# Zero rows under short k and v tiles, a third result buffer, and a new order of first loads in a linear-attention and softplus kernel

## The chip, the cores and the metric

The kernel runs on one NeuronCore of a Trainium2 chip. The metric is the device time of one execution in microseconds (us), the median of several runs. The engines are called PE (TensorE), DVE (VectorE), ACT (ScalarE), POOL (GpSimd) and SP (SyncE, which issues the DMA transfers).

## The reference

```python
batch, n_heads, seq, head_dim = (8, 8, 576, 64)

def attn(q, k, v, g_norm):
    kv = np.einsum('bhsd,bhse->bhde', k, v)
    out = np.einsum('bhsd,bhde->bhse', q, kv)
    rms = np.sqrt(np.mean(out * out, axis=-1, keepdims=True) + 1e-06)
    return out / rms * g_norm

def moe(x, w_in, w_out):                 # 4608 tokens, 512 -> 2048 -> 512
    h = x @ w_in
    g = np.maximum(h, 0.0) + np.log1p(np.exp(-np.abs(h)))
    return g @ w_out
# x is attn's output as (batch*seq, heads*dim); w_in and w_out are float64
```

A batch has 576 rows, that is four times 128 and 64 more. These 64 are the "tail" below.

## The kernel before

The program is written as tasks with an engine, an assumed duration, what they follow, which buffers of a ring they take and give back, and a priority number `pos`. Before anything is emitted, a list planner plays the tasks through with the assumed durations and fixes the order of every engine's queue:

```python
first = min(at for at, _ in options)
at, t = min(((at, t) for at, t in options if at <= first + self.SOON),
            key=lambda o: (o[1].pos, o[0]))        # the smallest pos among those that can start soon
```

On the chip each queue is worked off in that order.

The priorities of the first loads and conversions come from one list of 24 numbers:

```python
P0 = [-16.0, -13.7, -11.8, ...]
CONVERT, FETCH, EARLY = P0[:8], P0[8:16], P0[16:]
```

The sum over rows of k by v, per batch, with the tail as its last group:

```python
for p in range(NP + 1):
    ks, vs = slot("kvt"), slot("kvt")
    tail = p == NP
    ...
            if tail:
                l, r = pairs(ks.tile[:n], i), vs.tile[:n, 2 * i:2 * i + 2]     # n = 64
            else:
                l, r = pairs(ks.tile, i), vs.tile.rearrange("s (h i) d -> s h i d", h=2)[:, :, i]
            nc.tensor.matmul(kv[:, i if tail else p], lhsT=l, rhs=r, ...)
    last = add("PE", 1080 if tail else 820, run, ...)
```

After the attention rows come 192 steps (12 blocks of 384 tokens by 16 blocks of the hidden size, in three phases). Each step has 12 products `h`, a softplus, and 9 products `s`. Float32 factors are split in three parts for accuracy. At the end of a block the result tiles leave:

```python
ot = slot("xg" if ph == 0 else "qT")       # a ring of two
```

## Time and profile before

| | before |
|---|---|
| median, 3 runs | 940.94 us |
| median, the 6 runs timed with the changed kernel | 941.95 us |
| span of the profiled run | 942.6 us |
| PE busy | 921.1 us |
| PE idle ahead of the last matmul, of it ahead of the first | 16.2 us, 9.0 us |
| last matmul to the end | 5.2 us |

PE is the bound, and the lines of it stand in the prediction. To read them: "L544" is a line of the program, `h<-xv,w` gives the written and read tiles, and a fp32 matmul of the program shows as two instructions, so the four products of a k-by-v group are "x8".

### The profile page before, as it was taken

To read this page: it belongs to the slowest core of one execution; us is meant where nothing else is said; L and a number is where in the kernel's file an instruction comes from. 1 tells how busy PE (TensorE), PEld (TensorE's weight loads), DVE (VectorE), ACT (ScalarE), POOL (GpSimd) and SP (SyncE) were. 2 spreads that over 40 slices of the span, in tenths; PEclk is the share of its full clock that TensorE was granted. 3 is DMA by queue.
4 is the path that set the end of the run, shared out by engine and by line. 5 is a ranking of instruction groups with operands and counts; after the bars stand their busy time and mean duration, and the time that the engine had idled before them with its cause. 6 is when DMAs were issued, how large, how long until landed. Compare 5 with 4: busy or idle time off the path is not lost.

```text
span 942.6 us, 13502 instructions
## 1 busy us (share of the span) xinstructions
PE 921.1 (98%) x4978; PEld 834.6 (89%) x4978; DVE 597.9 (63%) x1043; ACT 447.7 (47%) x871; POOL 66.7 (7%) x42
## 2 busy tenths in 40 slices
PE   4899999999999999999999999999999999999997
PEld 3799899998989899899899999999999999999996
DVE  7788876677777646677666666485455454544452
ACT  6777666665565554544443333374323323233231
POOL 0322212122222000000000000000000000000000
PEclk9899999999999999999999999999999999999999
DMA  9998778857654433433333343343333322322321
GB/s 241 230 254 226 208 211 227 231 172 217 188 180 156 145 124 123 146 123 114 137 121 122 125 141 102 135 146 101 101 101 101 101 101 102 101 82 83 98 72 68
DMA packets 148673, 135.63 MB, mean 144 GB/s; under 512 B 86400, under 2 KB 102784, under 8 KB 148608
## 3 DMA queue, kind: packets, MB, share of 16 engines
q1 hardware_dynamic: 148448, 134.78, 47.0%
q8 instruction: 39, 0.64, 0.4%
q14 instruction: 26, 0.21, 0.1%
q10 hardware_dynamic: 160, 0.00, 0.0%
HBM read 93.85 MB, written 40.89 MB: 143 GB/s over the span
## 4 chain that ended last, share of the span: by engine, by line
PE 96%; DMA 2%; SPq 1%; DVE 0%; ACT 0%; issue 0%; POOL 0%; DVEq 0%; POOLq 0%
PE h L544 42%; PE s L551 42%; PE o L458 4%; PE o L482 3%; PE tp L498 2%; PE tp L476 2%; DMA x<-xg 1%; DMA q<-in_q_dram 1%; DMA kvt<-in_v_dram 1%; PE s L482 0%; SPq L442 0%; DMA out_dram<-qT 0%; POOL r L490 0%; SPq L444 0%; PE h L343 0%
## 5 line engine op out<-in xcount | busy, mean ns | idle before, releaser
L551 PE MATMUL s<-w,gv 128*128 128x512 f32 x1728 | 438.0, 396 | 0.3 <-ACT xg L585 0.3
L544 PE MATMUL h<-xv,w 128*128 128x384 f32 x2304 | 435.2, 337 | 0.0
L544 PEld LDWEIGHTS h<-xv,w 128*128 128x128 f32 x2304 | 405.0, 188 | 14.0
L551 PEld LDWEIGHTS s<-w,gv 128*128 128x128 f32 x1728 | 318.4, 188 | 59.1 <-ACT xg L585 0.6
L564 ACT ACTIVATE g<-h 128x384 f32<-128x384 f32 x192 | 94.2, 491 | 381.3 <-PE h L544 381.0
L555 DVE TENSOR_TENSOR gv<-g,gv 128x384 fp32r<-128x384 f32 x192 | 106.6, 555 | 180.2 <-ACT gv L566 179.6
L559 DVE SCALAR_TENSOR_TENSOR gv<-gv 128x384 fp32r<-128x384 f32 x192 | 107.0, 557 | 5.5
L566 ACT ACTIVATE gv<-g 128x384 fp32r<-128x384 f32 x192 | 100.9, 525 | 5.2
L400 DVE TENSOR_TENSOR xv<-xt,xv 128x512 fp32r<-128x512 f32 x102 | 70.1, 688 | 25.6 <-ACT xv L397 25.3
L490 POOL TENSOR_TENSOR r<-r,half 128x8 f32<-128x8 f32 x36 | 66.0, 1834 | 233.5 <-DVE r L487 233.5
L397 ACT ACTIVATE xv<-xt 128x512 fp32r<-128x512 f32 x102 | 63.6, 624 | 29.7 <-DMA xt<-x 29.7
L403 DVE SCALAR_TENSOR_TENSOR xv<-xv 128x512 fp32r<-128x512 f32 x108 | 74.5, 690 | 2.9
L458 PE MATMUL o<-kvt,kvt 128*128 128x128 f32 (+1 forms) x320 | 46.2, 290 | 10.9 <-DMA kvt<-in_v_dram 10.8
L458 PEld LDWEIGHTS o<-kvt,kvt 128*128 128x128 f32 (+1 forms) x320 | 42.9, 202 | 15.0 <-issue 13.3
L591 DVE SCALAR_TENSOR_TENSOR qT<-s,scale,kvt 128x512 f32<-128x512 f32 x36 | 26.9, 749 | 44.7 <-PE s L551 29.8
L591 DVE SCALAR_TENSOR_TENSOR qT<-s,kvt 128x512 f32<-128x512 f32 x36 | 24.8, 688 | 33.9 <-PE s L551 25.9
L482 PE MATMUL o<-kv_diag,qT 128*128 128x128 f32 (+1 forms) x296 | 37.0, 277 | 0.0
L482 PEld LDWEIGHTS o<-kv_diag,qT 128*128 128x128 f32 (+1 forms) x296 | 34.3, 179 | 1.2 <-issue 1.0
L486 DVE TENSOR_REDUCE r<-x 128x8 f32<-128x512 f32 x36 | 24.6, 685 | 14.1 <-ACT x L506 13.8
L501 ACT COPY qT<-tp 128x512 f32<-128x512 f32 x36 | 21.0, 583 | 18.8 <-PE tp L476 18.6
L512 ACT ACTIVATE xg<-tp,g_col 128x512 f32<-128x512 f32 x36 | 24.7, 686 | 9.0 <-PE tp L498 8.2
L493 DVE TENSOR_TENSOR x<-o,r 128x512 f32<-128x512 f32 x33 | 22.7, 687 | 7.0 <-POOL r L490 6.7
(61 smaller groups left out, 456.2 us busy)
## 6 DMA issues: line engine op xcount, KB each, us to landing
xt<-x SPq DMA_DIRECT2D x102, 256.0 KB, 3.3
kvt<-part SPq DMA_DIRECT2D x72, 256.0 KB, 4.0
kvt<-in_k_dram SPq DMA_DIRECT2D x72, 128.0 KB, 3.9
x<-xg SPq DMA_DIRECT2D x36, 256.0 KB, 3.1
part<-xg SPq DMA_DIRECT2D x36, 256.0 KB, 3.3
part<-qT SPq DMA_DIRECT2D x36, 256.0 KB, 2.1
out_dram<-qT SPq DMA_DIRECT2D x36, 256.0 KB, 3.1
raw<-in_moe_w_in_dram SPq DMA_DIRECT2D x16, 512.0 KB, 5.1
```

The source lines that it names most:

```text
L397: nc.scalar.activation(cols(0, F32R), x.tile, func=AF.Copy, scale=DOWN)
L400: nc.vector.tensor_tensor(out=cols(1, F32R), in0=x.tile, in1=cols(0), op=ALU.subtract)
L403: nc.vector.scalar_tensor_tensor(out=cols(2, F32R), in0=cols(1), scalar=-RADIX, in1=cols(0), op0=ALU.mult, op1=ALU.add)
L458: nc.tensor.matmul(kv[:, i if tail else p], lhsT=l, rhs=r, start=(p == 0 and i == 0), stop=tail, skip_group_check=True)
L482: nc.tensor.matmul(pairs(y[r0:r0 + n], p), lhsT=qT.tile[:, p, r0:r0 + n], rhs=kv_diag[b % 2][:, p], start=(p == 0), stop=True, skip_group_ ...
L490: nc.gpsimd.tensor_tensor(out=r.tile, in0=r.tile, in1=half, op=ALU.pow)
L544: nc.tensor.matmul(hp, lhsT=w_in.tile[:, i, kd * P:(kd + 1) * P], rhs=xv.tile[:, i, kd], start=(m == 0), stop=(m == 3 * KD - 1))
L551: nc.tensor.matmul(mine[i].tile, lhsT=gv.tile[:, m, i * P:(i + 1) * P], rhs=w_out.tile[:, m], start=(c == cs[0] and m == 0), stop=(c == cs ...
L555: nc.vector.tensor_tensor(out=gv.tile[:, 1], in0=g.tile, in1=gv.tile.bitcast(F32)[:, 0], op=ALU.subtract)
L559: nc.vector.scalar_tensor_tensor(out=gv.tile[:, 2], in0=f32[:, 1], scalar=-RADIX, in1=f32[:, 0], op0=ALU.mult, op1=ALU.add)
L564: a = add("ACT", 490, lambda: nc.scalar.activation(new(g, [P, NT]), h.tile, func=AF.Softplus, scale=1.0 + E), [a], s, [g], [h])
L566: a = add("ACT", 530, lambda: nc.scalar.activation(new(gv, [P, 3, NT], F32R)[:, 0], g.tile, func=AF.Copy, scale=DOWN), [a], s, [gv])
```

## The change

The intent: the tail's tiles get buffers of their own whose lower 64 rows are zero, so that all products have 128 rows; the last phase gets three result buffers in place of two, by borrowing from two idle rings; and the 24 priorities are chosen anew. The core of the diff (cuts at "..."):

```diff
-    P0 = [-16.0, -13.7, -11.8, -9.7, -5.1, 0.0, -13.9, 2.7, -33.5, -33.3, -24.2, -17.7, -12.2, -10.2, 15.3, -2.2, 1.5, -10.5, 6.5, 7.0, 5.0, 4.0, 4.5, 6.5]
+    P0 = [-61.0, -9.7, -13.3, -2.2, -4.6, 5.5, -46.9, 0.2, -37.5, -33.8, -28.2, -10.7, -14.2, -13.7, 28.3, -2.7, 1.0, -9.0, 6.5, 7.0, 7.0, 20.0, -0.5, 2.5]
+    tails = [const.tile([P, H, D], F32, name=f"tail{i}") for i in range(2)]
+                 tail0=1, tail1=1, ...                       # two more rings
-            d4 = add("DVE", 430, power, [d3], pos, [p])
+            d4 = add("DVE", 430, power, [d3], pos, [p, w])
-            ready = add("DVE", 690, total, [d3, d5], pos, [w], [t, p])
+            ready = add("DVE", 690, total, [d3, d5], pos, [], [t, p])
-            ks, vs = slot("kvt"), slot("kvt")
+            ks, vs = (slot(f"tail{i}" if tail else "kvt") for i in range(2))
...
-                        l, r = pairs(ks.tile[:n], i), vs.tile[:n, 2 * i:2 * i + 2]
+                        l, r = pairs(ks.tile, i), vs.tile[:, 2 * i:2 * i + 2]
-            last = add("PE", 1080 if tail else 820, run, lds + [last], pos + 0.5 * p,
+            last = add("PE", 820, run, lds + [last], pos + 0.5 * p,
-        ot = slot("xg" if ph == 0 else "qT")
+        ot = slot("xg" if ph == 0 else ("qT", "x", "q")[t % TB] if ph == LAST else "qT")
-    for kvd in kv_diag:
-        nc.vector.memset(kvd, 0.0)
+    for x in kv_diag + tails:
+        nc.vector.memset(x, 0.0)
```

More of the change, by code (lines that the diff above doesn't have):

```diff
@@ L190 @@
     rings = dict(xv=2, gv=3, g=2, raw=2, lf=1, sq=2, t=1, p=1, w=1,
-                 xt=2, kvt=6, q=2, qT=2, x=2, xg=2, r=2,
+                 tail0=1, tail1=1, xt=2, kvt=6, q=2, qT=2, x=2, xg=2, r=2,
                  h=2, o=2, tp=1, s0=1, s1=1, s2=1)
@@ L429, in kv_of @@
         for p in range(NP + 1):
-            ks, vs = slot("kvt"), slot("kvt")
             tail = p == NP
+            ks, vs = (slot(f"tail{i}" if tail else "kvt") for i in range(2))
             n = S - MAIN if tail else P
             def load(src, s, p=p, tail=tail, n=n, ks=ks):
+                if tail:
+                    s.tile = tails[s is not ks]
+                    nc.sync.dma_start(out=s.tile[:n], in_=src[b, :, MAIN:].rearrange("h s d -> s h d"))
+                    return
                 x = new(s, [P, H, D])
-                if tail:
-                    nc.sync.dma_start(out=x[:n], in_=src[b, :, MAIN:].rearrange("h s d -> s h d"))
-                    return
                 src = src[b, 2 * p:2 * p + 2, :MAIN].rearrange("h (s i) d -> s h i d", i=4)
```

## The prediction

> **What bounds the kernel now.** I read the page first, then TensorE's waits, then a table of stretches, then the chain of waits in order of time at the places that the change touches.
>
> The page's head:
>
> ```profile
> PE 921.1 (98%) x4978; PEld 834.6 (89%) x4978; DVE 597.9 (63%) x1043; ACT 447.7 (47%) x871; POOL 66.7 (7%) x42
> ...
> PE 96%; DMA 2%; SPq 1%; DVE 0%; ACT 0%; issue 0%; POOL 0%; DVEq 0%; POOLq 0%
> ```
>
> TensorE (PE) is busy for 921.1 of 942.6 us, and it makes up 96% of the chain that ended last. A busy PE alone would not prove a bound, but the chain agrees. So the change can win in three ways only: fewer PE nanoseconds, less of the 942.6 - 921.1 = 21.5 us in which PE stands idle, or less PE work done at a low clock. Where those lie, the table of stretches says (I cut it at PE's first matmul, at the changes of the granted clock and at the first matmul of the main loop; columns: PE, PE weight loads, DVE, ACT, POOL, clock, DMA share, GB/s):
>
> ```profile
> 0.00:8.96 8.96, 0.00 (x1) 0.03 (x1) 5.29 (x13) 5.16 (x9) 0.70 (x6) 1.00 0.75 209
> 8.96:14.30 5.34, 4.75 (x18) 3.96 (x18) 4.95 (x9) 2.32 (x6) 0.00 (x0) 1.00 1.20 281
> 14.30:21.20 6.90, 3.64 (x22) 2.65 (x22) 5.35 (x9) 6.10 (x13) 0.00 (x0) 1.00 1.27 249
> 21.20:31.40 10.20, 9.92 (x39) 8.56 (x40) 5.45 (x11) 5.78 (x13) 1.28 (x1) 0.50 1.18 269
> 31.40:44.50 13.10, 10.28 (x82) 8.90 (x80) 12.32 (x23) 10.75 (x21) 6.27 (x4) 1.00 0.79 206
> 44.50:75.00 30.50, 30.50 (x207) 28.19 (x206) 24.75 (x46) 21.91 (x45) 5.41 (x4) 1.00 0.99 241
> 75.00:300.00 225.00, 224.68 (x1412) 205.49 (x1412) 168.26 (x304) 147.53 (x287) 52.19 (x29) 1.00 0.69 202
> 300.00:937.00 637.00, 637.00 (x3206) 576.83 (x3205) 370.27 (x631) 248.16 (x486) 0.84 (x1) 1.00 0.34 112
> ```
>
> From 44.5 to 937 us PE never waits except for 0.32 us. All idle time is at the two ends: 8.96 us before the first matmul, 0.59 + 3.26 + 0.28 + 2.82 = 6.95 us between there and 44.5 us, and some 5 us after the last matmul. The stretch 21.2 to 31.4 is full of matmuls, but at clock 0.50: 9.92 us there are some 5 us of work at full clock. The first stretch of matmuls is slow as well, though its clock column says 1.00 (the record of the clock begins later): the chain puts 2.06 us on its first group of eight k-by-v instructions, against 0.89 us for the same group later.
>
> **What the Trainium skill says.** "TensorE: Matmul & The Clock Gate", Part 1: the clock is halved by default and after idle windows, and some 3.4 us of sustained activity releases it; the idle-to-slow step is the hazard. The trace agrees in kind: 2.06 against 0.89 us per group, 0.50 after the sparse stretch 14.3 to 21.2 (3.64 busy of 6.90). The same page, "LDWEIGHTS (loading the stationary operand)", says that a load's time goes by columns and not by the contraction's rows, so padding 64 rows to 128 should add nothing to a load; and Part 2, step 1, that weight loads are pulled ahead of running matmuls if row groups do not conflict or a background buffer takes them. It says nothing of a cost where 64-row and 128-row operations meet; the trace has one, below. "DMA: Bandwidth & Descriptors", "Specifications": pieces under 512 B are below the size for line rate. The page of the profile counts 86,400 of 148,673 packets under 512 B (q, k, v are read in 256 B pieces), and the start moves 209 to 281 GB/s with DMA shares of 0.75 to 1.27, so the first 31 us are fed by a saturated queue. I found no page that prices the planner's order.
>
> **Part 1: the padded tails.** Each batch's last 64 rows make four products of 64x128 by 64x128, two instructions each. The chain of waits around two of them, and one full group before them for the scale (start, us, what):
>
> ```profile
> 170.27 0.89 PE o L458 x8
> 171.16 2.09 PE h L544 x12
> 173.25 1.09 PE o L458 x8
> 174.34 0.59 PE tp L498 x4
> ...
> 96.67 1.08 PE o L458 x8
> 97.75 2.29 PE s L551 x9
> ```
>
> The full group of eight takes 0.89 us, the 64-row group 1.09, although half the rows are in use: +0.20. The group just after pays too: transposes 0.59 instead of 0.44 us (+0.15), nine s matmuls 2.29 instead of 2.10 (+0.19). Per batch that is 0.35 to 0.39 us; I take 0.37. The tails lie on a PE without gaps for seven of the eight batches, so all of it counts: 8 x 0.37 = **2.9 us saved** (batch 0's may partly drown in the start's idle time). My reading is that going from 128 rows to 64 and back spoils the overlap of weight loads, and zero rows make all operations alike.
>
> It adds two memsets of 128x512 on DVE; the two for kv_diag take 0.485 us each, so 0.97 us. DVE stands idle before its first conversion (1.77 us of waiting for the first weight, ended at 4.67 us), so they are hidden. The DMAs keep their bytes. The tails leave the kvt ring (six places, one of them held by a block of ones from 2.7 to 616 us), so that two of ten loads of each batch no longer wait for it. Above 44.5 us PE does not wait for loads, so that is worth nothing there.
>
> **Part 2: three result buffers in the last phase.** The end of the chain:
>
> ```profile
> 933.16 2.83 PE s L551 x12
> 936.00 0.03 issue
> 936.02 0.76 DVE qT L591
> 936.79 0.02 issue
> 936.80 2.03 DMA out_dram<-qT
> 938.83 0.03 issue
> 938.86 0.05 DVEq L591
> 938.91 0.04 issue
> 938.96 0.75 DVE qT L591
> ```
>
> The third result tile of the last block waits for the first tile's store, since the ring has two places. PE's last matmul ends at about 937.4 and DVE sits 1.48 us before 938.96. With a third buffer that operation starts at about 937.5, and its store (2 to 3 us, the page's median is 3.1) ends the kernel that much sooner: **1.4 us saved**. The other eleven blocks of the phase win nothing: DVE's wait for stores there is 12.0 us in all, with PE never idle.
>
> **Part 3: new places for first loads and conversions.** The weights' conversions and the loads are ordered by priority numbers; the new ones move batch 0's k and v, tails included, ahead of the q tiles (lead 20 instead of 4 steps), put the first w_in chunk's conversion first of all, and push weights 2 and 3 of phase 0 and later q and kv loads closer to use. Before the first matmul nothing changes that I can see: w_in, w_out, k, v are still the first four transfers, and v lands at 8.8. After it, in the old order, the tail's v is issued at 16.67 and the tail's products run at 23.35; q tiles and two 512 KB weights are issued in between. With tails in buffers of their own they can go at about 9, when the queue stalls for a kvt place (v's third load is issued only at 11.04). The fourth v load lands near 19, so batch 0's sum may be ready near 22 to 23 instead of 26.3, and the norm chain of the first three tiles, which opens the main loop at 44.5, moves by some 3 us.
>
> What this is worth is not those 3 us but what PE's idle and slow time shrink by, since PE's work is the same: at most 6.95 us of gaps plus about 5 us at half clock plus some 2.5 us of slow matmuls before 14.3, together 14.5. The loads' rate stays, so I guess that about 3 of the 7 us of gaps go and 1 us of the clock's loss on average: **4 us saved**, with a spread of +-4. This is the guess in the sum; the two others are readings.
>
> **Sum.** 2.9 + 1.4 + 4 = 8.3 us. 940.9 - 8.3 = 932.6 us, 0.9% less.
>
> **Rivals.** (a) *The clock takes it back.* If denser loads of kv leave PE sparser between its groups, the halved stretch lasts longer: each further 3.4 us at half clock costs 1.7 us. For it: the old stretch of half clock followed just such a sparse one. Then part 3 is 0 or below and the time is 936 to 940. (b) *The new order keeps PE fed from the first group on*, the clock never falls again, and most of the 14.5 us is won: 925 to 928. Against it: the first 31 us move 209 to 281 GB/s already, and the data needed does not shrink. (c) *Loads come too late later on.* q is now issued with a lead of 2.5 steps (about 10 us at 4.18 us per step) instead of 6.5, kv's lead falls too; landing takes some 4 us (medians 3.9 and 4.1), and the queue waits in order for other things for up to 18 us. PE waits of a few us, in several batches, between 50 and 250 us would eat the gain: 935 to 945. For it: DMA's share is 0.69 to 0.99 there. Against: a step has 4.18 us and the planner holds such orders to what frees when. (d) *The tail's extra is not due to the rows* but to the tail's layout; then part 1 gives nothing: 935.5.
>
> **Range and chances.** The sure parts give 936.6; rival (a) or (c) puts it up to 938, a lucky start down to 927. Faster by over 2% needs 922.1, more than (b) gives: 3%. Slower by over 2% needs 959.8, which only repeated waits in (c) could make: 1%. Within 2%: 96%.
>
> **What would show each step.** Right for part 1: 128-row tail groups at 0.89 us in the chain, and transposes after them at 0.44. Part 2: no DVE wait for a store before the last result, and the end some 4 us after the last matmul instead of 5. Part 3: the kv group of the tail before 23 us, the first main-loop matmul near 41, fewer us of idle PE before it and a shorter half-clock stretch. Wrong: new PE waits for q, kv or weights after 45 us, or a half-clock stretch as long as before or longer.

## The result, and the profile after

| | before | after |
|---|---|---|
| median, 6 runs each | 941.95 us | 941.0 us |
| lowest to highest | 940.32 to 943.34 us | 937.08 to 942.1 us |
| ratio, 95% interval | | 0.9985 (0.9963 to 1.0007) |

A ratio is the mean time of one kernel's runs over the mean of the other's in the same rounds. It is not quite the ratio of the medians, and plain means of all the runs listed differ from it by up to 0.0004. Where a difference in us is given with a ratio below, it is the ratio's distance from 1 times 942, about the mean of all runs of the kernel before. Here it is 1.4 us less, and the interval holds zero. The predicted 932.6 us, and the whole range of 927 to 938, lie below the median.

The profile taken of the changed kernel is its fastest run (937.08 us), and that of the kernel before was the slowest of all its runs (944.34 us). So the two traces differ by 7 us where the kernels differ by 1 or 2. What is the same in every run can be read from them; the start cannot.

The head of the page of the changed kernel, PE's busy time and its share of the chain:

```profile
PE 914.7 (98%) x4978; PEld 831.9 (89%) x4978; DVE 598.0 (64%) x1045; ACT 446.4 (48%) x871; POOL 66.2 (7%) x42
...
PE 96%; DMA 2%; SPq 0%; ACT 0%; issue 0%; DVE 0%; ACTq 0%
```

PE has the same 4978 instructions and stays the bound; it is busy for 6.4 us less. Part of that is padding and part is the clock of this run. The chain of waits of the changed kernel around a tail (the third line; the lines of the program have moved by two):

```profile
60.27 0.89 PE o L460 x8
61.16 0.70 PE s L553 x3
61.86 0.89 PE o L460 x8
62.75 0.70 PE s L553 x3
63.45 0.44 PE tp L500 x4
```

The tail's group takes 0.89 us like the full group above it, not 1.09, and nothing after it pays: three s products take 0.70 on both sides. The chain's end:

```profile
927.32 4.23 PE s L553 x18
931.55 0.02 issue
931.58 0.75 DVE q L593
```

The last DVE operation writes a buffer of the ring `q` and follows PE after 0.03 us; no store stands between. The span ends at 935.2, which is 3.7 us after PE, against 5.2 before.

The same stretches of the start as in the prediction, for the changed kernel:

```profile
14.30:21.20 6.90, 5.57 (x30) 4.88 (x30) 3.40 (x7) 3.43 (x8) 0.00 (x0) 0.75 1.17 284
21.20:31.40 10.20, 7.66 (x55) 6.38 (x55) 9.65 (x19) 9.13 (x18) 3.57 (x2) 1.00 1.26 238
31.40:44.50 13.10, 10.20 (x84) 8.72 (x83) 11.86 (x22) 10.59 (x21) 3.61 (x2) 1.00 1.07 263
44.50:75.00 30.50, 30.50 (x218) 29.27 (x217) 26.65 (x51) 23.80 (x47) 9.14 (x5) 1.00 1.01 254
```

In this run PE had the half clock for 3.4 us only and not for 10.2. Yet it stood idle for 16.8 us in all ahead of the last matmul, against 16.2, and the first product of the main loop starts at 44.72 us, against 44.47. The predicted gain at the start is not there even in the best run. (The profile of the kernel before is a late one in this too: in the runs below that keep its order, that product starts at 41.6 to 42.2 us.)

### The profile page after: what moved, and what is told of

Same layout as the page of the kernel before. It is cut to its first block, busy times and chain, and to the rows that moved or that the text cites. A ratio compares the mean times of both kernels' runs of the same rounds, so it can differ in the third digit from the quotient of the medians.

```text
span 935.2 us, 13489 instructions
## 1 busy us (share of the span) xinstructions
PE 914.7 (98%) x4978; PEld 831.9 (89%) x4978; DVE 598.0 (64%) x1045; ACT 446.4 (48%) x871; POOL 66.2 (7%) x42
## 4 chain that ended last, share of the span: by engine, by line
PE 96%; DMA 2%; SPq 0%; ACT 0%; issue 0%; DVE 0%; ACTq 0%
PE h L546 43%; PE s L553 43%; PE o L460 4%; PE o L484 3%; PE tp L500 2%; PE tp L478 2%; DMA q<-in_q_dram 1%; DMA kvt<-in_v_dram 1%; SPq L444 0%; PE s L484 0%; PE h L345 0%; PE h L344 0%; SPq L250 0%; DVE q L593 0%; ACT x L508 0%
## 5 line engine op out<-in xcount | busy, mean ns | idle before, releaser
L460 PE MATMUL o<-kvt,kvt 128*128 128x128 f32 x256 | 36.9, 292 | 11.4 <-DMA kvt<-in_v_dram 10.9
L460 PEld LDWEIGHTS o<-kvt,kvt 128*128 128x128 f32 x256 | 35.1, 206 | 12.9 <-issue 12.0
L488 DVE TENSOR_REDUCE r<-x 128x8 f32<-128x512 f32 x36 | 24.6, 683 | 6.3 <-ACT x L508 6.0
L593 DVE SCALAR_TENSOR_TENSOR qT<-s,scale,kvt 128x512 f32<-128x512 f32 x12 | 9.0, 751 | 29.5 <-PE s L553 29.5
```

What stands on the lines that cost most here:

```text
L460: nc.tensor.matmul(kv[:, i if tail else p], lhsT=l, rhs=r, start=(p == 0 and i == 0), stop=tail, skip_group_check=True)
```

## The experiments

Fifteen kernels ran, each in five rounds beside the kernel before; every one gave a correct result. The theory after the first result (A): padding and buffers are worth what was read from the trace, 2.9 and 1.5 us, and the new order of the start takes some 3 us back. The rivals (B) stand with each run.

### One part at a time

**tails_only**: the change with the old `P0` and the old `ot` line. It keeps the joint take of `p` and `w`, of which more below.

> The padded tails alone, old order, old result buffers. Theory A (each part is worth what was read, and the new order of the start takes back some 3 us): 2.9 us less than before (939.0 if before is 941.9), tail groups of 0.89 us and transposes after them of 0.44 us in the chain of waits. Theory B (the tails' gain is not there, or is given back by loads): within 1 us of before.

Measured: 948.56 us, ratio 1.0065 (1.005 to 1.008), so 6.1 us *more*. Both theories are wrong about this run.

**end_only**: the kernel before with the new `ot` line alone.

> The three result buffers alone. Theory A: from the last matmul's end to the end of the span 3.7 us instead of 5.2, so 1.5 us less than before (940.4). Theory B (the last store is bound by something else in most runs): no change within 0.5 us.

Measured: 939.8 us, ratio 0.9977 (0.9962 to 0.9993), 2.2 us less; theory A's direction, with somewhat more than the 1.5 us that were read.

**order_only**: the kernel before with the new `P0` and the joint take of `p` and `w`.

> The new places of loads and conversions alone (with the joint take of the two conversion buffers, which belongs to them). Theory A: some 3 us more than before (945), with more idle or half-clock time of TensorE before the main loop in a typical run. Theory B (the order is worth the 4 us that were predicted): 938. Theory C (the order moves nothing in the mean): 942 within 1 us.

Measured: 950.36 us, ratio 1.0088 (1.0071 to 1.0105), 8.3 us more.

**no_order**: the changed kernel with the old `P0`.

```diff
-    P0 = [-61.0, -9.7, -13.3, ...]
+    P0 = [-16.0, -13.7, -11.8, ...]
```

> The changed kernel with the old order put back: tails and result buffers together. Theory A: 2.9 + 1.5 = 4.4 us less than before (937.5), so 3 us below the changed kernel as well. Theory B: 941, like the changed kernel.

Measured: 947.72 us, ratio 1.006 (1.0045 to 1.0075), 5.7 us more. The buffers are worth only 0.5 us here (1.0065 - 1.006). No theory foresaw this run or the size of order_only's loss.

So padding with old priorities loses 6 us, new priorities without padding lose 8, and both together with the buffers win a little. The parts cannot be added. The reason is the planner: shorter tails and other rings give it another problem, and `P0` was fitted to one. Comparing the programs, tails_only leaves the order before at the fifth group of matmuls on PE. PE's timeline in tails_only shows where its 6 us are (start, us, engine, line):

```profile
64.49 3.73 PE L553 MATMUL s<-w,gv 128*128 128x512 f32 x15
...
83.36 1.16 PE L484 MATMUL o<-kv_diag,qT 128*128 128x128 f32 x8 [1.03 <-DVE x L495]
85.68 0.66 PE L500 MATMUL tp<-ident_r,x 128*128 128x128 f32 x4 [1.16 <-ACT qT L503]
...
90.24 2.35 PE L546 MATMUL h<-xv,w 128*128 128x384 f32 x12
```

Between 68.2 and 90.2 us no product of the main loop runs. PE works through attention rows one by one and waits for DVE and ACT between them. The `h` products at 90.24 need the fourth block of w_in, whose load is issued only at 69.15 us in this kernel, behind that of a block that the second phase needs (66.83); in the kernel before it is issued at 50.88 us.

### The parts with the order of instructions held

**pad_same_plan**: padding with the planner kept blind to it (the diff is cut at "...", and its two memsets are left out). It still sees the ring `kvt` and 1080 ns, so the order of PE, ACT, POOL and SP is that of the kernel before, entry by entry (DVE has two memsets more).

```diff
+    tails = [const.tile([P, H, D], F32, name=f"tail{i}") for i in range(2)]
-                x = new(s, [P, H, D])
                 if tail:
-                    nc.sync.dma_start(out=x[:n], in_=...)
+                    s.tile = tails[s is not ks]
+                    nc.sync.dma_start(out=s.tile[:n], in_=...)
                     return
+                x = new(s, [P, H, D])
-                        l, r = pairs(ks.tile[:n], i), vs.tile[:n, 2 * i:2 * i + 2]
+                        l, r = pairs(ks.tile, i), vs.tile[:, 2 * i:2 * i + 2]
```

> Padded tails with the instruction order of the kernel before kept on every engine (the planner still sees the old ring and the old 1080 ns for a tail; two memsets are added). Theory A (the padding itself is worth what was read, and the 6 us lost with the tails alone came from the new order that the planner made of them): 2.9 us less than before in the same clock state, tail groups 0.89 us, no new waits. Theory B (zero rows or the separate buffers cost something themselves): at or above before.

Measured: 939.87 us, ratio 0.9967 (0.9951 to 0.9983), 3.1 us less. The same padding that lost 6 us wins 3 when the order stays.

**pad_end**: the same with the new `ot` line.

> The same with the three result buffers of the last phase. Theory A: 2.9 + 1.5 = 4.4 us less than before, so about 937.5, and below the changed kernel (941) by 3. Theory B: like the changed kernel.

Measured: 938.08 us (937.49 to 939.41), ratio 0.995 (0.9935 to 0.9966), 4.7 us less.

**after_64rows**: the changed kernel, its order kept, with 64-row operands in the tail's products.

```diff
-                        l, r = pairs(ks.tile, i), vs.tile[:, 2 * i:2 * i + 2]
+                        l, r = pairs(ks.tile[:n], i), vs.tile[:n, 2 * i:2 * i + 2]
```

> The changed kernel, order the same on every engine, but the tail's products read 64 rows again. Theory A: 2.9 us more than the changed kernel, some 944. Theory B (padding is worth nothing): the same as the changed kernel.

Measured: 943.72 us, ratio 1.0012 (0.9995 to 1.003).

**after_again**: the changed kernel in the same rounds.

> The changed kernel again, on the same chip as the three others, for a second profile of its start. Theory A (its new order costs some 3 us at the start in a typical run, and its first profile was a lucky one): 940 to 942, with TensorE's idle time and half-clock time up to the last matmul some 3 us above the first profile's. Theory B: 937, like its first profile.

Measured: 940.85 us (939.92 to 941.75), ratio 0.9978 (0.9963 to 0.9994), 2.1 us less.

These four shared a chip and rounds. Padding is worth 3.1 us in the old order and 1.0012 - 0.9978 = 0.0034 or 3.2 us in the new. The buffers are worth 0.9967 - 0.995 = 0.0017 or 1.6 us. The new order against the old one, with padding and buffers in both, costs 0.9978 - 0.995 = 0.0028 or 2.6 us, and the two kernels' runs do not overlap. Theory A holds for all four in the time; for after_again it also foretold some 3 us more of idle and half-clock time than in the first profile, and there were 0.3 us more idle time and 10.2 us more at half clock.

### Where the new order loses 2.6 us

The stretches of pad_end, old order:

```profile
14.30:21.20 6.90, 4.07 (x23) 3.11 (x24) 5.83 (x11) 6.08 (x13) 0.00 (x0) 0.88 1.26 251
21.20:31.40 10.20, 10.01 (x60) 8.93 (x59) 7.05 (x15) 7.23 (x16) 2.67 (x2) 0.75 1.15 273
31.40:44.50 13.10, 10.31 (x73) 8.88 (x73) 12.37 (x23) 9.96 (x19) 4.68 (x3) 1.00 0.95 244
```

and of after_again, new order:

```profile
14.30:21.20 6.90, 5.11 (x22) 4.69 (x23) 3.21 (x6) 3.03 (x7) 0.00 (x0) 0.62 1.18 273
21.20:31.40 10.20, 8.01 (x37) 6.76 (x36) 7.11 (x14) 7.12 (x15) 1.75 (x1) 0.67 1.08 215
31.40:44.50 13.10, 10.40 (x80) 9.46 (x79) 10.44 (x20) 9.57 (x19) 4.09 (x3) 0.94 0.85 224
```

The new order has the lower clock in all three (0.62, 0.67, 0.94 against 0.88, 0.75, 1.00), and PE starts fewer matmul instructions between 14.3 and 31.4 us (22 + 37 = 59 against 23 + 60 = 83). The records give 13.7 us at half clock against 6.8 at the start, and PE idle for 17.2 us against 15.7. One profile each proves little, since the lengths at half clock vary from profile to profile, in steps of 3.4 us. But each run's mean clock is recorded: 0.9976 over the 11 runs of end_only and pad_end (old order, three buffers), and 0.9949 over the 17 of the three kernels with the new order and three buffers. Twice the missing share of some 938 us is 4.4 and 9.6 us at half clock, a difference of 5 us, or 2.6 us lost if all of it were full of work. That is an upper estimate: two of pad_end's five runs show 1.000, which can hide a slow start (see the closing list), and not all half-clock time is full of work.

The idle time is steadier than the clock. Ahead of its last matmul PE is idle for 15.7 to 16.5 us in the four profiles of the old order (before, end_only, pad_same_plan, pad_end) and for 16.8 to 17.2 us in the three of the new (after, after_64rows, after_again). So on average 0.8 us of the 2.6 is idle time; the next runs ask whether the rest is the clock.

**after_warm** and **pad_end_warm**: matmuls without data to wait for, ahead of the first groups, to hold the clock up.

```diff
             def run(...):
+                if b == 0:
+                    if p == 0:
+                        idle.append(ps.tile([P, d_model], F32, tag="s2_0", name="s2_0"))
+                    for _ in range((48, 0, 8, 8, 4)[p]):
+                        nc.tensor.matmul(idle[0][:, :P], lhsT=ident_r, rhs=ident_r, start=True, stop=True)
```

> The changed kernel with 48 products of the identity with itself before the first k-by-v group (TensorE stands idle there for 7 us) and 8, 8 and 4 before the third and fourth group and the tail; they read nothing that is loaded and write a bank not yet in use. Theory A (of the new order's 3 us, some 2 are half-clock time of TensorE and 1 to 1.5 more idle time): the half-clock time at the start goes, 3 to 5 us less than the changed kernel (936 to 938). Theory B (the clock has no part in it): 940 to 941, or more by the added work.

> The same fillers in the kernel with padded tails, three result buffers and the old order (938.1 without them). Theory A: it has less half-clock time to lose, so 1.5 to 3 us less (935 to 936.5), and the difference between the two orders shrinks from 2.7 to 1 to 1.5 us. Theory B: the difference stays 2.7 us.

Measured: 942.31 us, ratio 0.9996 (0.9982 to 1.0009), and 941.21 us, ratio 0.9986 (0.9973 to 0.9998). Both times are a miss, and the experiment's own fault, as PE's timeline of after_warm shows:

```profile
1.62 10.50 PE L458 MATMUL s<-ident_r 128*128 128x128 f32 x48 [1.62 <-DVE ident_r L625]
11.92 3.65 PE L466 MATMUL o<-kvt,kvt 128*128 128x128 f32 x16
```

The fillers ran until 11.9 us, 3 us past the arrival of the data, and did not even release the clock: the two groups after them still took 3.65 us. The difference between the two orders did shrink, to 0.001 or 0.9 us, as theory A had it; in both profiles the clock fell once, for 3.4 us, and PE was idle for 8.9 us in the new order against 7.9.

**after_q_first**: the changed kernel with the first q tile's load, transposes and copy moved back ahead of the tail's loads and of the third k-by-v group.

```diff
-    for t in plan.order():
+    tasks = plan.order()
+    for task, before in ((q_first[0], tail_loads[0]), (q_first[1], kv_runs[2]), (q_first[2], kv_runs[2])):
+        tasks.remove(task)
+        tasks.insert(tasks.index(before), task)
+    for t in tasks:
         t.run()
```

> The changed kernel with one thing of the old order put back: the load, the transposes and the copy of the first q tile stand ahead of the tail's loads and of the third k-by-v group, as before; all else keeps its place. Theory A (the hole of 2.3 us before the third group and the idle window after it come from q having been moved out of it): the hole falls to about 1.3 us, the time by 1 to 2 us (939 to 940). Theory B (the loads' rate alone sets the start): no change.

Measured: 942.23 us, ratio 0.9998 (0.9984 to 1.0011). No gain; if anything it is slower than the changed kernel. PE's hole of 2.3 us became two of 1.26 and 1.14, because v's third load landed later behind q. So the order of q alone is not the cause.

**pad_end_warm2** and **after_warm2**: mended fillers, 384 columns wide, from a buffer of the ring `gv` that is not yet in use.

```diff
+                    for _ in range((20, 0, 6, 5, 3)[p]):
+                        nc.tensor.matmul(idle[0], lhsT=ident_r, rhs=fill[:, 0], start=True, stop=True)
```

> Mended fillers: the first ones took 219 ns each, ran until 11.9 us and so delayed the first k-by-v group by 3 us, and did not release the clock. Now 20 products of 384 columns before the first group, and 6, 5 and 3 in the gaps, in the kernel with padded tails, three buffers and the old order. Theory A (half-clock time at the start is what the runs differ by): the first group runs at full clock, under 1 us instead of 2; 935 to 937 against 938.1. Theory B (the load queue sets the start, the clock is hidden behind it): 938 or more.

> The same fillers in the changed kernel (940.9 without). Theory A: the loss of the new order by the clock (some 5 us at half clock more than in the old order, so 2.6 us) is gone: 936 to 938, within 1.5 us of the same fillers in the old order. Theory B: the difference between the orders stays at 2.7 us or more.

Measured: 937.27 us, ratio 0.9948 (0.9935 to 0.9961), and 938.61 us, ratio 0.9962 (0.9946 to 0.9979). PE's timeline of pad_end_warm2:

```profile
2.02 5.54 PE L458 MATMUL s<-gv,ident_r 128*128 128x384 f32 x20 [2.02 <-DVE gv L628]
8.90 1.13 PE L466 MATMUL o<-kvt,kvt 128*128 128x128 f32 x8 [1.34 <-DMA kvt<-in_v_dram]
10.76 1.13 PE L466 MATMUL o<-kvt,kvt 128*128 128x128 f32 x8 [0.72 <-issue]
...
14.62 0.66 PE L484 MATMUL tp<-ident_r,q 128*128 128x128 f32 x4 [2.27 <-DMA q<-in_q_dram]
```

Now the first group runs at full clock, 1.13 us instead of about 2, and from 6 us on the record shows no half-clock stretch until after the last matmul. The difference between the orders falls to 0.9962 - 0.9948 = 0.0014 or 1.3 us. In the old order the full clock wins almost nothing (0.9948 against 0.995), as theory B had it: PE then waits longer for loads, 2.27 us for q ahead of 14.62, where in pad_end it waited 1.28 us ahead of 14.45. In the new order it wins about 1.5 us (0.9962 against 0.9978), though these two ratios come from different chips and their intervals overlap. So about half of the new order's cost is likely half-clock time. The other half stays with the clock held up: PE is idle for 13.1 us against 12.1 in these two profiles, and in the new order's the clock still fell once, for 3.4 us. The split is rough: from the scatter of the runs, the difference between the orders is uncertain by 0.5 us without fillers and by 0.6 with them (standard errors). Which loads make the rest is open.

### Why the parts cannot be added

**tails_fetch**: tails_only with one number of `P0` changed.

```diff
-    ... -10.2, 15.3, -2.2, ...
+    ... -10.2, -4.0, -2.2, ...
```

> The padded tails alone with one priority changed: the load of the fourth w_in block has -4.0 instead of 15.3, which puts it at place 38 of the queue instead of behind place 50, and the product that needs it at PE place 60 instead of 88. Theory A (the tails alone lost 6 us because the planner, given shorter tails and other rings, put that load at 66.8 us, and no product of the main loop ran between 68 and 90 us): the 5.9 us of idle TensorE between 60 and 100 us fall below 1, and the time falls from 948.4 to 939 to 942. Theory B (the separate tail buffers themselves cost the 6 us): 946 or more.

This text gives 66.8 us for the load in tails_only; that is the load ahead of it, and the fourth block's own is at 69.15, as said above. Measured: 940.43 us, ratio 0.9985 (0.9971 to 0.9998). The stretch from 60 to 100 us, first in tails_only, then in tails_fetch (the first number after the comma is PE's busy time of 40 us):

```profile
60.00:100.00 40.00, 34.14 (x234) 30.48 (x233) 31.54 (x58) 28.09 (x55) 12.42 (x7) 1.00 0.72 198
```

```profile
60.00:100.00 40.00, 39.15 (x256) 35.95 (x255) 32.53 (x58) 28.08 (x55) 10.99 (x6) 1.00 0.82 226
```

5.86 us of idle PE became 0.85, and with them 7.5 us of the time went (1.0065 to 0.9985). So it was the place of one load in the queue, and not the buffers. A shift of one priority re-plans what follows as well, so the 7.5 us are not this load's wait alone.

Two more things can be read from the planner by itself, played through without the chip (its times are sums of the assumed durations, so estimates). First, the joint take of `p` and `w`, which tails_only has and pad_same_plan has not, has no run of its own. With it alone, the kernel before keeps its order on every engine; without it, the planner gets stuck on the numbers of tails_only and of order_only. So it is no rival cause of the 6 us. Second, the loss stood in the plan. The planner's own end of the program is 941.6 us for the kernel before, 940.5 with the shorter tail alone, 945.2 with the two rings alone, 950.6 with both (tails_only, measured 948.56), 947.8 for order_only (950.36), 942.3 for tails_fetch (940.43) and 937.8 for the changed kernel (941.0). It also puts the first product of the main loop at 42.6 us before and at 45.1 after.

**tails_fetch_end**: the same with the new `ot` line.

> The same with the three result buffers: 1.5 us less than the run before, so 938 to 940 under theory A, beside 938.1 for the old order with padded tails and three buffers.

Measured: 939.35 us, ratio 0.9965 (0.9949 to 0.998), 3.3 us less than before. It is a good version, but pad_end with 0.995 is not beaten.

The best kernels are pad_end and pad_end_warm2. pad_end changes the old kernel in the padding and the buffers alone; at 938.08 us it is below both the kernel before and, in shared rounds, the changed kernel. What the fillers add to it is too small to be told.

## Why the prediction was wrong

**The bound** was read rightly: PE in both kernels, with no idle time above 45 us that loads would cause.

**Part 1, padding** was right. 2.9 us were predicted; 3.1 and 3.2 us were measured with the order held in both orders. The groups fell from 1.09 to 0.89 us and what follows them no longer pays. The reading of why, a spoilt overlap of weight loads, fits the single instructions of the traces: in the kernel before, a weight load starts 3 ns (median) after the start of the product ahead of it, but at the changes between 128 and 64 rows after 45 us it starts 200 to 318 ns after it. Inside the 64-row group it is 3 ns again, and in pad_same_plan it is 2 or 3 ns at the same places. The memsets were hidden as said: DVE still waited 0.87 us for the first weight. Rival (d), that the rows are not the cause, is refuted by after_64rows.

**Part 2, buffers** was right: 1.4 us predicted, 1.5 in the profiles, and 1.6, 1.9 (tails_fetch_end) and 2.2 in the runs; only no_order, with 0.5, shows less.

**Part 3 failed**, and with it the sum. The step was "I guess that about 3 of the 7 us of gaps go and 1 us of the clock's loss on average: 4 us saved". Measured is a cost of 2.6 us. The tail's group did come earlier, as foretold (19.5 and 20.4 us in the two profiles, before 23), but the first product of the main loop did not move to 41: it started at 44.7 and 49.1. The gaps did not close: PE's idle time ahead of the last matmul is longer than in the profiles of the old order, by 0.3 to 1.5 us. And rival (a) came about in part: the fillers took 1.3 of the 2.6 us away, so about half of the cost is likely half-clock time, and after_again has 13.7 us of it where the kernel before had 10.2, one of the prediction's own signs of being wrong. The prediction named this rival and gave it too little weight. What makes the rest of the cost stays open beyond the longer idle time.

**The deeper error** is in the sum itself. It took the new priorities as a gain of their own on top of the other two parts. They are a repair: padding as the planner sees it throws the old order off by some 9 us (from 0.9967 with the order held to 1.0065; with the three buffers, from 0.995 to 1.006, some 10 us), and the new numbers win back all but 2.6 of that. The diff showed it: 1080 had become 820 and two loads had left the ring, in a program whose order is planned from just these numbers. A priority list that changes together with a duration is no sign of a better start. The plan could have been played through before the prediction, and it has the main loop start 2.5 us later.

**Rival (c)**, loads too late above 45 us, did not happen in the changed kernel; PE was idle for 0.0 us from 60 to 300 us in both profiles. It did happen in tails_only. In order_only PE stood idle for 4.0 us between 60 and 75 us, but what it waited for in the end was not followed up. **The interval** was too narrow also because one profile stood for the start: the runs of the kernel before spread from 940.3 to 944.1 with the clock, and the profile of it that the prediction rests on was slower still, at 944.34.

## What to carry to other kernels

Where the order of queues comes from a planner, test a change with the order held before testing it with the order new: the same padding won 3 us in one and lost 6 in the other. Retuned constants in a diff may pay for the rest of it, so don't count them as a gain until they are measured alone and together. A planner that is plain code can be run before the chip is: here it foretold which mixtures would lose. Where one engine is the bound, operations of odd shape can cost their neighbours time too, and zero rows that need no transfer may be the cheaper form.

## What the Trainium skill lacked or had wrong

- "TensorE: Matmul & The Clock Gate", "LDWEIGHTS (loading the stationary operand)", says that the rows do not matter for the time of a weight load. For the load itself the trace agrees: 188 ns with 64 rows in after_64rows, 192 with 128. What is lacking is the cost where the rows change: a load there started 200 to 318 ns after the product ahead of it and not 3, four products of 64 rows took 1.09 us against 0.89, and the operations after them 0.15 to 0.2 us more; padding them with zeros won 3.1 us in eight batches. The page to which this belongs, "TensorEngine Tiling (Array Packing)", "Key Properties", says that a change of tiling mode drains the engine. It gives no time for it, and no run here shows whether 64 rows are such a mode.
- "TensorE: Matmul & The Clock Gate", Part 1, gives some 3.4 us of sustained activity for the release of the clock. 48 matmuls of 128 columns, back to back for 10.3 us, did not release it (the next two groups took 3.65 us, and the record's first full clock came at 15.4 us); 20 of 384 columns, from 2.0 us on, did by 6.0 us. Both multiplied an identity by identities. What counts as activity these two runs do not settle. Nor did the clock need an idle window to fall, as the page has it: in the kernel before it fell at 21.15 us, after 3.41 us in which PE was busy for 1.13, and PE's longest hole since its first matmul was 1.66 us. The stretches at half clock did come in steps of 3.41 us (3.41, 6.83, 10.24), as the page's window has it.
- No page that was read says that in a profile like these the clock counts as full until the first record of it. In tails_fetch_end it stood at 1.00 from 14.3 to 21.2 us, and a k-by-v group there took about 2 us, as at half clock; the first record of full clock came at 24.6 us. A mean clock of 1.000 can therefore hide a slow start.
